# Block-sparse attention and a gated feed-forward layer on one core: weight rows in whole transfers, later loads in one piece, a new order

## The chip, the cores and the metric

The kernel runs on one core of one Trainium2 chip. A core has a tensor engine (PE, with its weight load shown apart as PEld), a vector engine (DVE), a scalar engine (ACT), GpSimd (POOL) and SyncE (SP), and sixteen DMA engines that serve all of them. The metric is the device time of one execution in microseconds (us). Three runs of the kernel before took 331.52, 333.68 and 333.03 us: the median is 333.03.

## The reference

```python
# q, k, v: (4, 8, 768, 64) f32: batch, heads, sequence, head size; blocks of 32
scores = scale * np.matmul(q, k.transpose(0, 1, 3, 2))
mask = np.abs(blk_i - blk_j) <= 1          # neighbours
mask = mask | (blk_i == 0) | (blk_j == 0) | (blk_i == n_blocks - 1) | (blk_j == n_blocks - 1)
for qb in range(n_blocks):                  # and three sampled blocks for each block of queries
    for kb in sampled_blocks[qb]:
        mask[qb*32:(qb+1)*32, kb*32:(kb+1)*32] = True
attn = softmax(np.where(mask, scores, -1e9))
x = np.matmul(attn, v)  # -> (3072 tokens, 512)
gate = 1.0 / (1.0 + np.exp(-(x @ w_gate)))  # w_gate, w_val: (512, 1536)
out = gate * (x @ w_val) @ w_out            # w_out: (1536, 512), out: (3072, 512) f32
```

## The kernel before

**Attention.** The four batches follow one another. For each, q, k and v are loaded with a cast from f32 to f16 into a ring of five staging buffers (`stg`). Such a cast is asked of POOL's DMA queue (q0 in the profile). Batch 0's are cut in few pieces; for batches 1 to 3 `load` (L551) cuts each of the three into `LPARTS = 4` transfers of two heads, 192 KB each as written. From batch 1 on k and q are put in row order by a copy on POOL or DVE (L726, L728); q's load is issued after k's copy, since the ring has no more room (L732). PE transposes k and q (L747, L750), and ACT and DVE evict them into `KT` and `QT` (L760, L765, L767). v is put in row order by DVE (L777) and stored to scratch in DRAM (`scr`, L786, on SP's queue from batch 1 on). From there windows of neighbouring blocks (L819) and the sampled blocks (L892, three gathers of 32 KB for each block of queries, on SP's queue, with registers for the block numbers) come back into `V1` and `V2`. The first and last block are held in `FL` and copied in (L831, L833).

A step handles two blocks of queries for all eight heads: POOL gathers their keys into `KG` (L868, L879), PE computes the scores (L912 for the mask, L919), DVE the maxima (L928), ACT the exponentials (L940), DVE the reciprocals (L947) and DVE or ACT the scaling (L960, L963); PE transposes the weights (L974), ACT or DVE evicts them (L980), PE multiplies by V (L993), and ACT or DVE evicts to `XA` (L1009, L1014). Eleven steps make a batch; the first and last block, which see all keys, are four dense units (L648, L1044 to L1098).

**Feed-forward.** The 24 tiles of 128 tokens are taken in seven groups: groups 0 and 1 have two tiles each, all of batch 0; group 2 has the last two tiles of batch 0 and the first two of batch 1; and so on. For each of twelve slices of 128 of the 1536 columns PE makes a gate matmul and a value matmul of four each (L1136, over the four parts of 128 of the 512 inputs), ACT takes tanh (L1144), and DVE combines (L1149). Then twelve matmuls with `wo` make a tile of the output (L1171), evicted at L1178 or L1180 and stored on SP's queue (L1185).

**Weights.** `weights` (L570) loads `wg` and `wv` in four column chunks of 384 columns, each in two transfers of 192 KB as written (L580), gate and value in turn; then `wo` in three parts of two transfers (L589). A gate matmul of a slice waits for the gate and the value chunk that hold that slice (L1139, L1141).

**The order.** All work is a list of operations with engines, costs, dependencies, buffers to take and to give back, and a priority. A planner (`Planner.run`, L196) sets them in order by list scheduling: for each engine the operation that can begin first, and among those about equal the one of lowest priority number. The kernel then issues the operations in that order, each engine in its own. `OFFSETS` shifts priorities by kind of operation, batch and quarter of the batch; `PREP` says when a batch's preparation comes; `DENSE` when the dense units. `GATES` names weight transfers that are issued only after the gathers of a block of batch 0 have been issued; `LGATE` does so for the loads of a batch, which wait for the gathers of that block of the batch before (L1107 to L1111). `FETCH` is what the planner reckons for one piece of PE's code while POOL's queue is loaded and while it isn't. Where PE has nothing to do before 60 us the planner puts in dummy matmuls (L1205).

Of the kernel before, what the change touches and what calls it, by code (L numbers as in the profile page):

```python
# [33 lines left out]
PREP = [-50.0, 0.26, 10.34, 20.82]  # L34


GATES = {0: 4, 4: 9, 6: 5, 8: 9}


LGATE = {1: 18, 2: 11, 3: 13}  # L40
# [27 lines left out]
}  # L68


def kind(o):

# [99 lines left out]
class Planner:  # L172
# [8 lines left out]
    LANES = 8  # L181


    PIECE, FIRST, FETCH = 256, 150, {True: 5.2, False: 3.5}

    def __init__(self):
        self.ops = []
# [167 lines left out]
def kernel(  # L355
# [15 lines left out]
    def pin(x):  # L371
        return tc.keep_in_program_order(x)
# [883 lines left out]
```

## Time and profile before

| | |
|---|---|
| median of three runs | 333.03 us |
| the profiled execution | 332.75 us |
| its span, first to last instruction | 331.0 us |
| PE busy | 311.0 us (94%) |
| DVE busy | 237.1 us (72%) |
| ACT busy | 219.0 us (66%) |
| POOL busy | 127.4 us (38%) |
| mean granted clock of PE | 0.983 |
| q0 (POOL's queue) | 17984 packets, 16.39 MB |
| q1 (SP's queue) | 24628 packets, 24.83 MB |
| q8 (PE's code) | 36 packets, 0.59 MB |

Busy tenths cut the span in 40 equal slices of 8.3 us; a digit is the busy share in tenths. "PEclk" is the granted clock of PE in tenths. In tables of stretches the share of DMA adds up the queues, so that it can pass 1. A row of the timeline or of waits names the engine and line that waited and, behind an arrow, what released it. The chain of waits is followed back from the last instruction; "issue" there is time in which nothing that the profile shows was waited for. Times to landing run from the issue of a transfer to its completion. The profile is of one execution, and the sums are made against its 332.75 us; 1.75 of them lie outside the span.

### The profile page before, as it was taken

The numbers are of one execution on the slowest core, as the hardware profiler recorded it, in microseconds if no ns is written. First come the engines' busy times: TensorE is split into PE (matmuls) and PEld (weight loads), VectorE is DVE, ScalarE is ACT, GpSimd is POOL, SyncE is SP. The second block draws the span as 40 slices with busy tenths as digits, with TensorE's granted clock in tenths as the row PEclk, the third lists the DMA queues.
The fourth block names the chain that finished last, engine by engine and source line by source line (L and its number), as shares of the span: only waits on it lengthen the run. The fifth ranks groups of instructions, "written<-read, shape, count | busy, mean of one in ns | idle before, by whom it ended". The sixth has DMA issues, their size and how long they took to land.

```text
span 331.0 us, 12430 instructions
## 1 busy us (share of the span) xinstructions
PE 311.0 (94%) x4574; PEld 188.7 (57%) x4574; DVE 237.1 (72%) x533; ACT 219.0 (66%) x656; POOL 127.4 (38%) x373
## 2 busy tenths in 40 slices
PE   6988898897997999999999999999999999999996
PEld 2545577766855746655556565655655665444443
DVE  3399987853697898998899976788987986304310
ACT  2156987854569999875895975759988765223322
POOL 6497786555445666443462433152221000000000
PEclk9999999999898799999999999999999999999999
DMA  7959999978523979524369742462223310020002
GB/s 112 216 174 220 224 225 234 214 195 186 155 73 90 188 175 213 133 65 143 113 136 220 172 107 97 126 171 63 69 64 105 108 35 0 2 95 32 0 34 95
DMA packets 42672, 42.00 MB, mean 127 GB/s; under 512 B 6931, under 2 KB 38804, under 8 KB 42612
## 3 DMA queue, kind: packets, MB, share of 16 engines
q0 software_dynamic: 17984, 16.39, 30.3%
q1 hardware_dynamic: 24628, 24.83, 25.8%
q8 instruction: 36, 0.59, 0.8%
q14 instruction: 24, 0.20, 0.2%
HBM read 45.97 MB, written 9.44 MB: 167 GB/s over the span
## 4 chain that ended last, share of the span: by engine, by line
PE 74%; DVE 13%; ACT 7%; issue 3%; DMA 2%; SPq 0%; DVEq 0%; ACTq 0%
PE bank L1136 32%; PE bank L1171 18%; ACT P L940 4%; PE bank L993 4%; PE bank L974 4%; PE twin L919 3%; PE twin L1205 3%; DVE NM L928 2%; DVE HT L1149 2%; DMA V<-scr 2%; DVE P L963 2%; PE twin L912 2%; DVE V L831 1%; PE bank L1081 1%; PE bank L750 1%
## 5 line engine op out<-in xcount | busy, mean ns | idle before, releaser
L940 ACT ACTIVATE P<-twin,NM 128x256 f16<-128x256 f32 x176 | 81.5, 489 | 15.1 <-DVE NM L928 14.9
L1149 DVE SCALAR_TENSOR_TENSOR HT<-TH,bank 128x512 f16<-128x512 f32 (+1 forms) x84 | 51.1, 609 | 41.7 <-PE bank L1136 37.7
L1136 PE MATMUL bank<-XA,wv 128*128 128x512 f16 (+1 forms) x336 | 77.1, 352 | 1.6 <-issue 1.1
L1136 PE MATMUL bank<-XA,wg 128*128 128x512 f16 (+1 forms) x336 | 77.0, 352 | 0.2 <-ACT XA L1009 0.2
L868 POOL COPY KG<-KT 128x64 f32 x264 | 51.4, 246 | 57.2 <-PE twin L919 50.6
L1144 ACT ACTIVATE TH<-bank 128x512 f32<-128x512 f32 (+1 forms) x84 | 45.8, 546 | 31.8 <-PE bank L1136 30.7
L1171 PE MATMUL bank<-wo,HT 128*128 128x512 f16 (+1 forms) x300 | 64.8, 370 | 0.3 <-DVE YS L1178 0.3
L928 DVE TENSOR_REDUCE NM<-twin 128x4 f32<-128x1024 f32 x44 | 52.5, 1218 | 3.2 <-PE twin L919 1.9
L1136 PEld LDWEIGHTS <-wv 128*128 128x128 f16 x336 | 31.7, 99 | 27.4 <-issue 2.5
L1171 PEld LDWEIGHTS <-HT 128*128 128x128 f16 x300 | 28.7, 98 | 30.5 <-issue 0.6
L1136 PEld LDWEIGHTS <-wg 128*128 128x128 f16 x336 | 30.5, 99 | 22.7 <-issue 1.2
L940 ACT ACTIVATION_READ_ACCUMULATOR P<-twin,NM 128x1 f32 x176 | 39.0, 221 | 0.0
L963 DVE TENSOR_SCALAR P<-P,ZZ 128x256 f16<-128x256 f16 x134 | 32.1, 301 | 1.5
L993 PEld LDWEIGHTS <-V 128*128 128x128 f16 x704 | 26.3, 100 | 11.4 <-issue 5.2
L974 PEld LDWEIGHTS <-P 128*128 128x128 f16 x352 | 22.8, 99 | 9.8 <-issue 3.5
L974 PE MATMUL bank<-ident,P 128*128 128x128 f16 x312 | 24.7, 222 | 2.1 <-ACT XA L1009 0.8
L833 POOL COPY V<-FL 32x768 f32<-32x768 f32 (+1 forms) x18 | 16.0, 922 | 26.6 <-PE bank L993 13.5
L993 PE MATMUL bank<-PTS,V 128*128 128x64 f16 x512 | 21.9, 197 | 4.5 <-DMA V<-scr 2.3
L1180 ACT ACTIVATE YS<-bank 128x512 f32<-128x512 f32 (+1 forms) x15 | 8.5, 569 | 21.9 <-PE bank L1171 21.9
L960 ACT ACTIVATE P<-P,ZZ 128x256 f16<-128x256 f16 x42 | 19.1, 520 | 4.3 <-DVE ZZ L947 4.1
L980 DVE COPY PTS<-bank 128x1024 f16<-128x1024 f16 x25 | 17.1, 685 | 5.3 <-PE bank L974 5.3
L919 PE MATMUL twin<-KG,QT 64*32 64x160 f16 x704 | 19.1, 238 | 0.0
(88 smaller groups left out, 394.1 us busy)
## 6 DMA issues: line engine op xcount, KB each, us to landing
V<-scr SPq DMA_DIRECT2D x264, 32.0 KB, 2.7
out_dram<-YS SPq DMA_DIRECT2D x23, 256.0 KB, 2.1
V<-scr SPq DMA_DIRECT2D x14, 288.0 KB, 4.3
stg<-in_v_dram POOLq DMA_DIRECT2D x12, 192.0 KB, 5.3
stg<-in_k_dram POOLq DMA_DIRECT2D x12, 192.0 KB, 7.5
scr<-stg SPq DMA_DIRECT2D x3, 768.0 KB, 3.4
stg<-in_q_dram POOLq DMA_DIRECT2D x12, 192.0 KB, 6.6
V<-scr SPq DMA_DIRECT2D x6, 384.0 KB, 4.2
```

Of the source, the lines that this page charges most:

```text
L868: pin(nc.gpsimd.tensor_copy(t[:, :, 1 + n], KW[r][:, :, bass.ds(vals[(i % 8) * 3 + n], BLK // 2)]))
L919: pin(nc.tensor.matmul(t[hh][cs, u, c0:c1], QT[r][rs, p, BLK * i : BLK * i + BLK], src, start=False, stop=True, skip_group_check=True))
L928: pin(nc.vector.tensor_reduce(NM[o.slots[hz][1]][:, 0:4], t, axis=AX.X, op=ALU.max, negate=True))
L940: pin(nc.scalar.activation(pb[:, u, :], t[:, u, :], AF.Exp, bias=NM[z][:, x : x + 1], scale=1.0, accum_out=ZZ[z][:, x : x + 1]))
L960: pin(nc.scalar.activation(pb[:, u, :], pb[:, u, :], AF.Copy, scale=ZZ[z][:, 2 * hh + u : 2 * hh + u + 1]))
L963: pin(nc.vector.tensor_scalar(pb[:, u, :], in0=pb[:, u, :], scalar1=ZZ[z][:, 2 * hh + u : 2 * hh + u + 1], scalar2=None, op0=ALU.mult))
L974: pin(nc.tensor.transpose(t[:, c * 128 : c * 128 + 128], pb[:, c * 128 : c * 128 + 128], ident))
L993: pin(nc.tensor.matmul(t[:, u, p, :], vt[:, ws, p * 128 : p * 128 + 128], pt[:, u, c, :, 32 * p : 32 * p + 32], start=(c == 0), stop=(c == ...
L1136: pin(nc.tensor.matmul(t, wt[:, c, f_ * 128 : f_ * 128 + 128], XT[g][:, c, :], start=(c == 0), stop=(c == 3)))
L1144: pin(nc.scalar.activation(TH[o.slots[ht][1]][:, 0:n], banks[o.slots[hg][1]][:, 0:n], AF.Tanh, bias=0.0, scale=0.5))
L1149: pin(nc.vector.scalar_tensor_tensor(HT[:, f_, hoff : hoff + n], in0=TH[o.slots[ht][1]][:, 0:n], scalar=1.0, in1=banks[o.slots[hv][1]][:, ...
L1171: pin(nc.tensor.matmul(t, HT[:, f_, hoff + tt * 128 : hoff + tt * 128 + 128], wo[:, f_, cols], start=(f_ == 0), stop=(f_ == NF - 1)))
```

## The change

Gate and value weights are loaded by whole rows: for each of the four parts of 128 inputs, one transfer of 128 rows of 1536 columns (384 KB as written), first the four of `wg` and then the four of `wv`. Every gate matmul then waits for all eight, and every value matmul for the four of `wv`, since each slice of columns needs all four parts. `wo` is loaded in three transfers of 512 KB. Each of q, k and v of batches 1 to 3 is loaded in one transfer of 768 KB. The planner's costs for these and for code pieces are set anew, and so are `GATES`, `LGATE`, one value of `PREP` and many of `OFFSETS`, so that the order of the work on each engine is another.

```diff
-PREP = [-50.0, 0.26, 10.34, 20.82]
-GATES = {0: 4, 4: 9, 6: 5, 8: 9}
-LGATE = {1: 18, 2: 11, 3: 13}
+PREP = [-50.0, 0.26, 10.34, 20.76]
+GATES = {1: 6, 2: 7, 4: 9, 5: 7, 6: 5}
+LGATE = {1: 14, 2: 11, 3: 14}
...
 OFFSETS = {
...
-    PIECE, FIRST, FETCH = 256, 150, {True: 5.2, False: 3.5}
+    PIECE, FIRST, FETCH = 256, 150, {True: 7.0, False: 3.6}
...
-    WCH, WOH = 4, 3
+    WOH = 3
...
-    LPARTS = 4
-
...
                 if name == "v":
-                    pin(nc.gpsimd.dma_start(v_head(t)[:, z], src[b].rearrange("h (p j) d -> p h j d", j=VJ)[:, z]))
+                    pin(nc.gpsimd.dma_start(v_head(t), src[b].rearrange("h (p j) d -> p h j d", j=VJ)))
...
-        n = NF // WCH
-        for ch in range(WCH):
-            c0, c1 = ch * n * 128, (ch + 1) * n * 128
-            for nm, t, src in (("wg", wg, moe_w_gate), ("wv", wv, moe_w_val)):
-                def f(o, t=t, src=src, c0=c0, c1=c1):
-                    for z in (slice(0, 2), slice(2, 4)):
-                        pin(nc.gpsimd.dma_start(t[:, z, c0:c1], src[:, c0:c1].rearrange("(c p) n -> p c n", p=128)[:, z]))
-                prev = P(f"{nm}{ch}", "POOL", 1.5, f, prio=-30, dma=8.8 / WCH, ndma=2, after=[prev])
+        for nm, t, src in (("wg", wg, moe_w_gate), ("wv", wv, moe_w_val)):
+            for ch in range(4):
+                def f(o, t=t, src=src, ch=ch):
+                    pin(nc.gpsimd.dma_start(t[:, ch, :], src[ch * 128 : ch * 128 + 128, :]))
+                prev = P(f"{nm}{ch}", "POOL", 0.75, f, prio=-30, dma=6.8 / 4, after=[prev])
                 FF["gate"].append(prev)
-                for ff in range(ch * n, ch * n + n):
-                    res[nm, ff] = prev
+            FF[nm] = FF["gate"][-4:]
         n = NF // WOH
         for ch in range(WOH):
             def f(o, r0=ch * n, r1=ch * n + n):
-                for z in range(r0, r1, 2):
-                    pin(nc.gpsimd.dma_start(wo[:, z : z + 2, :],
-                                            moe_w_out[z * 128 : z * 128 + 256, :].rearrange("(c p) n -> p c n", p=128)))
-            prev = P(f"wo{ch}", "POOL", 1.6, f, prio=-30, dma=9.4 / WOH, ndma=2, after=[prev])
+                pin(nc.gpsimd.dma_start(wo[:, r0:r1, :],
+                                        moe_w_out[r0 * 128 : r1 * 128, :].rearrange("(c p) n -> p c n", p=128)))
+            prev = P(f"wo{ch}", "POOL", 0.85, f, prio=-30, dma=9.4 / WOH, after=[prev])
...
-            ldv, hv = load("v", v, b, pp - 0.050, ldeps, LPARTS)
-            ldk, hk = load("k", k, b, pp - 0.049, ldv[-1:], LPARTS)
-            ldq, hq = load("q", q, b, pp - 0.048, ldk[-1:], LPARTS)
+            ldv, hv = load("v", v, b, pp - 0.050, ldeps)
+            ldk, hk = load("k", k, b, pp - 0.049, ldv)
+            ldq, hq = load("q", q, b, pp - 0.048, ldk)
...
-                  deps=xdeps + [w["wg", f_], w["wv", f_]], prio=pr, count=4, ...
+                  deps=xdeps + FF["wg"] + FF["wv"], prio=pr, count=4, ...
-                   deps=xdeps + [w["wv", f_], a], prio=pr, count=4, ...
+                   deps=xdeps + FF["wv"] + [a], prio=pr, count=4, ...
```

More of the change, by code (lines that the diff above doesn't have):

```diff
@@ L558, in f @@
                 t = stg[pl.handles[h][1]]
-                z = QPARTS[x] if tokens else slice(x * n, x * n + n)
                 if name == "v":
-                    pin(nc.gpsimd.dma_start(v_head(t)[:, z], src[b].rearrange("h (p j) d -> p h j d", j=VJ)[:, z]))
+                    pin(nc.gpsimd.dma_start(v_head(t), src[b].rearrange("h (p j) d -> p h j d", j=VJ)))
                     return
                 t, y = by_head(t), src[b].rearrange("h (p j) d -> p h j d", j=TJ)
+                z = QPARTS[x] if tokens else slice(x * n, x * n + n)
                 pin(nc.gpsimd.dma_start(t[z], y[z]) if tokens else nc.gpsimd.dma_start(t[:, z], y[:, z]))
             res.append(P(f"ld{name}{b}{x}", "POOL", 0.8, f, after=list(after) + res[-1:], prio=prio,
-                         acq=[(h, stages)] if x == 0 else [], lat=LATE[0] if b else None, dma=4.4 * (QPARTS[x].stop - QPARTS[x].start) / TP if tokens else 4.4 / parts))
+                         acq=[(h, stages)] if x == 0 else [], lat=LATE[0] if b else None, dma=3.4 * (QPARTS[x].stop - QPARTS[x].start) / TP if tokens else 4.4 / parts))
         return res, h
@@ L1138 @@
             a = P(hg, "PE", n * 0.00168, lambda o, f_=f_, h=hg, fn=f_mm: fn(o, f_, h, wg),
-                  deps=xdeps + [w["wg", f_], w["wv", f_]], prio=pr, count=4, acq=[(hg, pg_of(g)), (ht + "t", [("ff", x) for x in range(len(pg_of(g)) // 3)])])
+                  deps=xdeps + FF["wg"] + FF["wv"], prio=pr, count=4, acq=[(hg, pg_of(g)), (ht + "t", [("ff", x) for x in range(len(pg_of(g)) // 3)])])
             b_ = P(hv, "PE", n * 0.00168, lambda o, f_=f_, h=hv, fn=f_mm: fn(o, f_, h, wv),
-                   deps=xdeps + [w["wv", f_], a], prio=pr, count=4, acq=[(hv, pg_of(g))], rel=[ht + "t"])
+                   deps=xdeps + FF["wv"] + [a], prio=pr, count=4, acq=[(hv, pg_of(g))], rel=[ht + "t"])
             def f_th(o, hg=hg, ht=ht, n=n):
```

47 rows, old and new, of the table OFFSETS are left out of this document.

## The prediction

> **What bounds the kernel now.** I read the busy tenths of the page first, then busy time by stage, then the chain of waits, the DMA queues by stage, and the timelines of POOL and SyncE.
>
> ```profile
> PE   6988898897997999999999999999999999999996
> PEclk9999999999898799999999999999999999999999
> DMA  7959999978523979524369742462223310020002
> ```
>
> PE is busy nearly throughout; its gaps, and both dips of the granted clock, lie in the first 15 slices of 8.3 us. DMA is full from slice 4 to slice 8 (25 to 66 us). By stage:
>
> ```profile
> 46.00:64.00 18.00, 15.82 (x354) 13.10 (x354) 14.18 (x36) 14.27 (x56) 12.73 (x41) 1.00 1.24 227
> ...
> 78.00:86.00 8.00, 5.75 (x51) 4.48 (x50) 1.88 (x6) 2.07 (x8) 5.19 (x17) 0.79 0.69 209
> ...
> 101.00:114.00 13.00, 9.88 (x294) 8.27 (x268) 11.03 (x27) 11.85 (x42) 9.88 (x32) 0.74 0.78 151
> ...
> 130.00:278.00 148.00, 147.64 (x2306) 88.17 (x2305) 126.53 (x277) 115.48 (x357) 46.71 (x159) 1.00 0.44 111
> ```
>
> The columns are the stretch, its length, busy time of PE, PEld, DVE, ACT and POOL, granted clock, DMA share (queues added) and GB/s. From 130 us on PE has nothing to give back: what is lost or won there must come from more or less work, and the change has none. The recoverable time lies ahead of it: 2.2 us idle in 46 to 64; 2.25 idle and 21% of the clock over 8 us (1.7) in 78 to 86; 3.1 idle and 26% over 13 us (3.4) in 101 to 114. That is some 12.7 us. Before 46 us PE waits for the first attention steps and is kept warm by 82 dummy matmuls (L1205); DVE is busy 24.4 of the 26 us from 20 to 46 and sets that pace.
>
> Why PE stands at 78 and 101:
>
> ```profile
> 59.09 1.05 issue
> ...
> 74.77 5.70 DMA V<-scr
> ```
> ```profile
> SPq L786 <- DVE P L963: 8.0, 1, 8.0
> ```
> ```profile
> 59.65 2.53 POOL L564 DMA_DIRECT2D stg<-in_k_dram  x4
> 69.52 1.90 POOL L726 COPY stg<-stg 96x2048 f32<-96x2048 f32 x1 [7.34 <-DVE P L963]
> 71.36 2.50 POOL L564 DMA_DIRECT2D stg<-in_q_dram  x4
> ```
>
> Batch 1 comes late. Its v is issued from 54.4 to 59.7 and lands about 65.3; SyncE holds the store of the shuffled v (L786) for 8.0 us, and behind it, in order, stand the last gathers of batch 0: a gather issued at 74.8 lands 5.7 us later and PE stands 2.25 us for it (the 78 to 86 hole). Batch 1's k lands about 69.4 (last quarter issued by 62.2, median 7.2 to landing), is shuffled at 69.52, q is issued behind that and shuffled at 81.21, and batch 1's first scores run at 91.1. By 101 the gate and value matmuls of groups 0 and 1 are used up, and those of group 2, which needs batch 1's tiles, begin at 113.6: the second hole.
>
> **The change, part by part.**
>
> *Weight rows.* The price of a packet, from the queue views of three stretches:
>
> ```profile
> q0 software_dynamic: 283, 0.90, 91.8%
> ...
> q0 software_dynamic: 1353, 0.98, 106.1%
> ...
> q0 software_dynamic: 1026, 0.88, 111.1%
> ```
>
> These are 23 to 27, 36 to 42 and 62 to 67 us. Share x length x 16 engines / packets gives 208 ns at 3.2 KB (V windows, no cast), 75 ns at 0.72 KB (weights, with some 4-byte completions) and 87 ns at 0.86 KB. In the packet records a 768 B weight piece takes 79 ns at the median and a 1 KB piece of k 97, so 18 ns for each further 256 B. A whole row is 3072 B written, so 97 + 8 x 18 = 241 ns is my estimate; ends 208 (the uncast row) and 316 (four times 79: no gain). Gate and value weights are 4096 pieces now, 4096 x 79 / 16 = 20.2 us of all engines; 1024 rows at 241 are 15.4. Saved: 4.8 us of a stage where DMA is full (0 to 6.9).
>
> *The new gate.* Every gate or value matmul now waits for all eight row transfers, where now the first needs two column chunks. The weights flow from about 28.3 us (mean packet size falls from 3.2 to 0.7 KB there) at q0 shares of about 1.05: 28.3 + 20.2/1.05 = 47.5 now, 28.3 + 15.4/1.05 = 43 after, and 1.5 us to the landing: 44.5. The first of these matmuls runs at 46.33 now, set by attention, so I cost the gate at nothing; its cover is 1.8 us. Without it (rows at 316 ns) they land at 49, a loss of up to 2.7. Queued behind a waiting matmul on PE would be batch 0's attention, hence the bound counts in full.
>
> *POOL's issues.* 16 weight issues at 0.71, 6 of wo at 0.70 and 36 quarter loads at 0.67 become 8, 3 and 9; the rows of larger transfers are 0.73 (384 KB, batch 0's k) and 0.92 (768 KB, its v), so 39.7 us become about 16. POOL is not the bound (50.6 us of its idle is waiting for score matmuls), and I count nothing for this by itself, but q of batch 1 is issued in one go of about 0.7 to 0.9 us and not in 2.5.
>
> *Batch 1 earlier.* Behind the weights in the same queue stand wo (1536 x 97/16 = 9.3 us), v (1024 x 79/16 = 5.1) and k (768 x 97/16 = 4.7), 19.1 in all. At 0.95 of the engines: 47.5 + 20.1 + 1.7 = 69.3, which is where k lands now, and 64.8 after. The gate on the loads moves from the gathers of block 18 to those of block 14, the eleventh block, gathered by about 41 us, so the loads can stand in the queue before wo is done. k, its shuffle, q and its shuffle come 4.5 us earlier, q 1 to 2 more for its single issue: 4.5 to 6. The SyncE store of v comes about 5 earlier, and with it the gathers behind it. The start of group 2 moves from 113.6 by about 5, since PE had slack there and DVE (11.0 of 13) and ACT (11.9 of 13) are what the first steps of batch 1 go by. Gain 5 us (0 to 12.7, the whole recoverable time). What is late next is those steps themselves on ACT and DVE.
>
> *Batches 2 and 3.* Same single transfers; PE is full there, so nothing (worth 0 either way while PE has work from earlier groups).
>
> *Longer packets beside others.* Small gathers landed in 6.4 us (median of 6) beside the 3.2 KB packets of 23 to 27 and in 4.5 (of 10) beside the 0.72 KB ones of 36 to 42. PE's code comes through the same engines: 36 pieces of 16 KB (q8), one per 254 PE instructions (9148/36). From 45.6 to 63.8 they came every 6.1 us, and PE stood for them in the middle of a run, 1.1 us at 52.9 and 1.05 at 59.1 ("issue"). Under weight rows, from 28 to 43, gathers and code may come 1.9 us later. The dummy matmuls and the DVE pace cover it in part: the third step's PV ran at 41.7, while its gathers were issued by 30. I take 0.5 us (0 to 3 there).
>
> The Trainium skill, DMA: Bandwidth & Descriptors, "Queues, rings and completion order", says that each engine takes turns between queues only at packet boundaries. It speaks against this change, and the 6.4 against 4.5 us agrees with it. By that rule alone the 1.9 us would stand once in full on the way to the first gate matmul, and the sum would be 330 where mine is 328.
>
> *The order.* Engine orders are replanned as a whole and can't be seen here; ±4 us, the size of one hole of the two.
>
> **Sum.** 332.75 (the profiled execution; span 331.0) - 5 + 0.5 = 328.25, say 328. The runs' median of 333.03 is 0.3 above the profiled one, which alters nothing. 1% is 3.3 us, about what can be told from no change.
>
> **Rivals.**
>
> *Code late (slower).* Place: 46 to 68, where PE already goes by its code pieces. If larger transfers hold each back by a further 1.9 us (the gathers' difference), four pieces cost 7 us, part regained from batch 1: 332.75 + 7 - 3 = 336 to 337. It decides once the spacing of pieces there exceeds 6.1 us. For: PE's two stalls lie exactly there. Against: by then the rows have landed, and wo and the loads keep their 1 KB and 768 B packets.
>
> *All weights too late.* Rows no faster than pieces: 2.7 lost at 46 and nothing gained for batch 1: 335. For: a cast row of 3 KB stands nowhere in the trace. Against: 208 ns for 3.2 KB uncast.
>
> *Hidden anyway.* Batch 1 is earlier, but ACT (11.9 of 13) holds its first steps, or the order gives the gain back: 330 to 335.
>
> *A new hole.* The new order lets PE run dry once more as from 101 to 114 (6.5 us), after 114, where nothing of batch 0 is left to fill it, and keeps 2 of the gain: 332.75 + 6.5 - 2 = 337. For: the planner counts costs, not this chip's waits. Against: PE idles 0.4 us in 148 from 130 on, with the gate work of a whole group in hand.
>
> *All of it.* Both holes close, the clock stays up, and the order uses it: 320 to 323.
>
> **Chances.** Forecast (325 to 331) 0.42; all of it 0.10; hidden 0.09; weights too late 0.05; code late 0.19; a new hole 0.15. Faster by over 1% (below 329.7) is all of "all of it" and 0.36 of the forecast: 0.46. Within 1%: the rest of the forecast, hidden, and a little of the weights and of code late: 0.18. Slower (above 336.3): 0.36. For 8 in 10 I leave out the near end of "all of it" beyond 321 and what lies above 339; that takes in the lost cover of the gate, code late, a new hole and most of the recoverable 12.7. Both signs hold much of the chance; the likeliest case's own range is 325 to 331.
>
> **What would show it.** Right: the weight packets at 3 KB and near 241 ns; the last weight landed by 45 and the first gate matmul by 47; batch 1's k shuffle near 65 and its first scores near 86; no clock dip near 82; group 2's first gate matmul near 108. Wrong: rows near 316 ns, code pieces over 6.1 us apart between 46 and 68 with "issue" on PE, or PE below full after 130.

## The result and the profile after

The changed kernel takes 334.04 us (median of 20 runs), the kernel before 331.81 in the runs beside it: a ratio of 1.0052, 95% interval 1.0027 to 1.0078. The ratio leaves out executions more than 1.5% above their kernel's fastest, so by it the change is slower by about 1.7 us and not by the 2.2 of the medians. 328 had been forecast; the measured change is inside the 1% that was named as about what can be told from no change. The profiled execution of the changed kernel took 336.02 us (span 334.1), 2 us above the median of its runs, which lie between 331.4 and 336.6, so single gaps below are read for what they are and not added up to the microsecond.

The page after, busy tenths in 40 slices of 8.35 us:

```profile
PE   5997697899899898999999979999999999999996
PEclk9999999999999999999999999999999999999999
DMA  7959999979329991434397934533223020020002
```

Both dips of the granted clock are gone (slices 11, 13 and 14 before), as forecast. That holds for this execution, whose mean granted clock was 0.998; over the twenty the mean lies between 0.990 and 1.000, mostly at 0.995, and over 25 of the kernel before, the base of e13 to e16, between 0.978 and 0.995. One stretch of 3.41 us at half clock, as the kernel before has one from 81.1 us on, takes 0.005 off the mean. But PE's row has new weak slices: the first, the fourth and the fifth, and slice 24, around 195 us, where the kernel before had nothing but nines. By stage, with the columns as before (stretch, length, busy time of PE, PEld, DVE, ACT and POOL, granted clock, DMA share, GB/s):

```profile
46.00:64.00 18.00, 15.52 (x344) 11.57 (x344) 15.42 (x41) 16.73 (x58) 3.89 (x14) 1.00 1.23 227
78.00:86.00 8.00, 6.92 (x83) 4.83 (x84) 4.93 (x8) 4.66 (x11) 3.49 (x3) 1.00 0.64 172
101.00:114.00 13.00, 12.96 (x178) 7.92 (x174) 10.70 (x27) 12.00 (x37) 2.83 (x13) 1.00 1.15 213
114.00:130.00 16.00, 14.09 (x262) 9.25 (x259) 12.62 (x26) 12.70 (x37) 9.18 (x31) 1.00 0.71 170
130.00:278.00 148.00, 144.13 (x2148) 83.78 (x2146) 121.40 (x273) 108.10 (x310) 41.12 (x142) 1.00 0.43 108
```

The two holes of before have closed: 78 to 86 went from 5.75 busy at a clock of 0.79 to 6.92 at 1.00, and 101 to 114 from 9.88 at 0.74 to 12.96 at 1.00. From 130 us on, where PE had been busy 147.64 of 148 us, it now stands for 3.9. What PE waits for from 110 to 200 us (engine, line and what released it: us in total, times, longest):

```profile
PE twin L1062 <- DVE DP L1053: 1.7, 1, 1.7
PE bank L741 <- POOL stg L720: 1.0, 1, 1.0
PE bank L1130 <- DVE HT L1143: 0.9, 1, 0.9
PE bank L741 <- DVE stg L722: 0.6, 1, 0.6
```

Lines of the changed kernel are six below those of the kernel before, up to the end of the file: L1130 is the gate and value matmul (L1136 before), L987 the product with V (L993), L913 the scores (L919), L720 GpSimd's copy of k or q into row order (L726), L862 the copy of keys (L868), L1053 the scaling of a dense unit (L1059). The four waits come, in this order, at 194, 115, 133 and 129 us.

The early part lost too. In the chain that leads to 54 us, pieces in order of time (start, us, what):

```profile
25.36 8.30 DMA V<-scr
...
38.31 0.10 PE twin L913 x11
38.40 1.56 issue
39.96 0.36 PE twin L913 x14
```

PE waits 1.33 us for the gather that takes 8.30 us to land, and stands 1.56 us in the middle of a run of scores: a piece of its code had come at 37.45 to 38.39. The stand ends 1.6 us after that piece's packet; others like it end 1.2 to 1.5 us after theirs, at 54.0 and 60.1 us in the kernel before, at 52.6 in the changed one and at 49.9 in e9. From 24 to 50 us the kernel before has neither wait. Milestones of five kernels, read from the first gate matmul of a group of tiles (the columns on the right are experiments, below):

| us | before | after | a third of the weights (e9) | short copies (e11) | both (e13) |
|---|---|---|---|---|---|
| first gate matmul | 46.3 | 49.0 | 46.3 | 48.5 | 46.5 |
| first scores of batch 1 | 91.2 | 86.9 | | | |
| group 2 begins | 113.6 | 110.4 | 108.2 | 108.9 | 107.6 |
| group 3 | 164.5 | 163.9 | 159.3 | 161.2 | 158.1 |
| group 4 | 210.8 | 213.0 | 208.4 | 209.7 | 205.6 |
| span | 331.0 | 334.1 | 329.4 | 330.2 | 326.1 |

So the changed kernel starts 2.7 us late, is 3.2 ahead at group 2, 0.6 ahead at group 3 and 2.2 behind at group 4. A milestone of one order doesn't stand for the same work done as in the other; PE's idle time, which "The sum, mended" adds up below, doesn't have this fault. The same early part also differs from execution to execution: in the changed kernel, e11, e14, e15 and e16, which are alike up to 68 us, the first gate matmul comes at 48.1 to 49.5. The question for the experiments is what makes the start late, and what takes the lead of group 2 away.

### The profile page after: what moved, and what is told of

The parts are those of the page before. It is cut to its first block, busy times and chain, and to the rows that moved or that the text cites. A ratio compares the mean times of both kernels' runs of the same rounds, so it can differ in the third digit from the quotient of the medians.

```text
span 334.1 us, 12372 instructions
## 1 busy us (share of the span) xinstructions
PE 310.6 (93%) x4577; PEld 186.9 (56%) x4577; DVE 236.1 (71%) x539; ACT 221.0 (66%) x647; POOL 103.0 (31%) x338
## 4 chain that ended last, share of the span: by engine, by line
PE 65%; DMA 12%; DVE 7%; ACT 7%; issue 4%; SPq 3%; POOL 1%; POOLq 0%; DVEq 0%; ACTq 0%
PE bank L1130 30%; PE bank L1165 14%; PE bank L987 4%; PE bank L968 4%; DMA V<-scr 4%; DMA stg<-in_q_dram 3%; ACT P L934 3%; SPq L886 3%; PE twin L913 3%; PE twin L1199 2%; PE twin L906 2%; DVE V L825 1%; DMA scr<-stg 1%; DMA out_dram<-YS 1%; DMA FL<-scr 1%
## 5 line engine op out<-in xcount | busy, mean ns | idle before, releaser
L1130 PE MATMUL bank<-XA,wv 128*128 128x512 f16 (+1 forms) x336 | 76.0, 348 | 2.3 <-DVE HT L1143 2.1
L862 POOL COPY KG<-KT 128x64 f32 x264 | 50.0, 243 | 90.7 <-PE twin L913 84.4
L1130 PE MATMUL bank<-XA,wg 128*128 128x512 f16 (+1 forms) x336 | 76.1, 349 | 1.0 <-ACT TH L1138 0.4
L1130 PEld LDWEIGHTS <-wv 128*128 128x128 f16 x336 | 31.4, 98 | 27.7 <-issue 3.2
L1130 PEld LDWEIGHTS <-wg 128*128 128x128 f16 x336 | 29.6, 98 | 23.1 <-issue 2.7
L957 DVE TENSOR_SCALAR P<-P,ZZ 128x256 f16<-128x256 f16 x146 | 36.8, 313 | 1.5
L987 PEld LDWEIGHTS <-V 128*128 128x128 f16 x704 | 26.1, 98 | 12.2 <-issue 5.9
L1174 ACT ACTIVATE YS<-bank 128x512 f32<-128x512 f32 (+1 forms) x19 | 10.9, 572 | 30.0 <-PE bank L1165 28.0
L987 PE MATMUL bank<-PTS,V 128*128 128x64 f16 x624 | 26.1, 193 | 3.1 <-DMA V<-scr 2.2
L968 PEld LDWEIGHTS <-P 128*128 128x128 f16 x352 | 22.2, 98 | 10.1 <-issue 2.9
L827 POOL COPY V<-FL 32x768 f32<-32x768 f32 (+1 forms) x20 | 18.5, 953 | 21.4 <-PE bank L987 13.2
L974 ACT COPY PTS<-bank 128x1024 f16<-128x1024 f16 x18 | 18.2, 1013 | 7.8 <-PE bank L968 7.7
L913 PE MATMUL twin<-KG,QT 64*32 64x160 f16 x704 | 19.2, 234 | 2.7 <-issue 2.7
L720 POOL COPY stg<-stg 96x2048 f32<-96x2048 f32 x5 | 9.4, 1890 | 38.6 <-PE bank L1075 16.8
```

The lines of the kernel that those rows point to most:

```text
L827: pin(nc.gpsimd.tensor_copy(dst.bitcast(f32), src.bitcast(f32).broadcast_to([BLK, n, DM // 2])))
L862: pin(nc.gpsimd.tensor_copy(t[:, :, 1 + n], KW[r][:, :, bass.ds(vals[(i % 8) * 3 + n], BLK // 2)]))
L913: pin(nc.tensor.matmul(t[hh][cs, u, c0:c1], QT[r][rs, p, BLK * i : BLK * i + BLK], src, start=False, stop=True, skip_group_check=True))
L957: pin(nc.vector.tensor_scalar(pb[:, u, :], in0=pb[:, u, :], scalar1=ZZ[z][:, 2 * hh + u : 2 * hh + u + 1], scalar2=None, op0=ALU.mult))
L968: pin(nc.tensor.transpose(t[:, c * 128 : c * 128 + 128], pb[:, c * 128 : c * 128 + 128], ident))
L987: pin(nc.tensor.matmul(t[:, u, p, :], vt[:, ws, p * 128 : p * 128 + 128], pt[:, u, c, :, 32 * p : 32 * p + 32], start=(c == 0), stop=(c == ...
```

## The experiments

Each run stands against runs of the kernel before on the same chip; ratios are to those, with 95% intervals. Where a run is set against the changed kernel, its ratio is divided by 1.0052; the intervals of both then count. The theories at the start were: the longer packets or transfers cost time by themselves (A, C); the order is what costs or gains (B); or both only in one another's company.

### Parts of the change, one at a time

**e1: the new order, weights in short packets.** The same eight transfers, cut by columns, so that packets are 768 B. Cut so, the first gate matmul and the first value matmul each wait for one transfer (landed at 33.7 and 43.2 us), so the new gate is out of this run as well.

```diff
-pin(nc.gpsimd.dma_start(t[:, ch, :], src[ch * 128 : ch * 128 + 128, :]))
+pin(nc.gpsimd.dma_start(t[:, :, ch * 384 : ch * 384 + 384],
+                        src[:, ch * 384 : ch * 384 + 384].rearrange("(c p) n -> p c n", p=128)))
```

> The changed kernel in its own order, its eight weight transfers of 384 KB kept in number and size, but each a chunk of 384 columns of all four parts, so that its packets are 768 B and not 3072 B as written. Theory A (long weight packets hold back the gathers and PE's code of batch 0, and move no more bytes per us): gathers issued from 28 to 36 us land in about 5.0 us and not 6.5, PE's 1.3 us wait for a gather at 33.8 goes, the first gate matmul comes 1 to 2 us before 49.0, and the time falls by 1 to 2.5 us, to about 332. Theory B (the new order is the cost, not the packets): the time stays at 334 within 0.7. The step of the prediction that rows are faster: the weights would take 4 to 5 us longer, the first gate matmul would come at 53 or so and the time would rise by 2 to 4.

1.0108 (1.0073 to 1.0142): 0.5% slower than the changed kernel, not faster. Its gathers of 28 to 36 us land in 5.1 us at the median, against 6.5 in the changed kernel, and the 1.33 us wait is gone, but the stand for code is still there (1.56 us at 37.2) and the first gate matmul comes at 49.5. In between lies a dip of the clock. The same six dummy matmuls, in the changed kernel and in e1:

```profile
40.71 1.46 PE L1199 MATMUL bank<-ident 128*128 128x512 f16 x6
```
```profile
39.65 2.77 PE L1199 MATMUL bank<-ident 128*128 128x512 f16 x6
```

Up to there e1 is 1.1 us ahead; from 39.4 to 42.8 us the granted clock stands at half, and the lead is gone. So long packets are what makes the gathers slow and not what makes the code late; whether the start would come earlier without them, this execution doesn't show. The run's time doesn't hang on such a dip alone: an execution at a mean clock of 0.999 took 336.25.

**e2: the new order, later loads in four transfers each.**

```diff
-pin(nc.gpsimd.dma_start(v_head(t), src[b].rearrange(...)))
+for y in range(4 if b else 1):     # two heads each; k and q likewise
+    pin(nc.gpsimd.dma_start(v_head(t)[:, s], src[b].rearrange(...)[:, s]))
```

> The changed kernel in its own order, but q, k and v of batches 1 to 3 each loaded in four transfers of 192 KB as before, issued one after the other at the same place. Theory C (single transfers of 768 KB are what delays batches 2 and 3): batch 2's q, issued at 116.3, lands in about 9 us and not 11.6, PE's idle time from 114 to 136 shrinks by 1 us or more, and the time falls by 1 to 2 us. Theory A and theory B: nothing but POOL's extra issue time of about 1.7 us for a load, so the time stays at 334 within 0.7, or rises by up to 1.

1.0071 (1.0045 to 1.0098), the same as the changed kernel within the intervals. Whole loads neither gain nor cost there.

**e3: the old order, later loads whole**, each issued in the place of its first quarter.

```diff
+if b:
+    if x:
+        return
+    z = slice(0, H)
```

> The kernel before in its own order, but q, k and v of batches 1 to 3 each loaded in one transfer of 768 KB, issued where the first quarter stood. Theory C: 1 to 2 us slower than before, ratio 1.003 to 1.006. Theories A and B: the same within 0.7 us, or a little faster, since POOL has 1.7 us less to issue for each load: ratio 0.997 to 1.001.

1.0022 (0.9982 to 1.0062): no difference that this can tell.

**e4: the old order, weights by rows.** Each of its eight weight operations issues one whole row transfer.

```diff
-for z in (slice(0, 2), slice(2, 4)):
-    pin(nc.gpsimd.dma_start(t[:, z, c0:c1], src[:, c0:c1].rearrange("(c p) n -> p c n", p=128)[:, z]))
+c = c0 // 384
+pin(nc.gpsimd.dma_start(t[:, c, :], src[c * 128 : c * 128 + 128, :]))
```

> The kernel before in its own order, but its eight weight operations each load one whole row of 1536 columns (one transfer of 384 KB with 3072 B packets, not two of 192 KB with 768 B), gate and value in turn; every gate matmul then needs all eight. Theory A: the gathers slow as in the changed kernel (6.5 us), the last weights land at 48 to 50, the first gate matmul, set at 46.3, waits until then and holds batch 0's attention behind it on PE: 2 to 4 us slower, ratio 1.006 to 1.012. Theory B: the gate falls in PE's slack, ratio within 1.002. The step of the prediction that rows are faster: the last weights land by 45, nothing waits, and the time falls by up to 2 us.

1.003 (1.0004 to 1.0057). Gathers of 28 to 36 us land in 8.0 us at the median where they took 5.0, those of 36 to 43 in 7.5 where they took 4.5. That agrees with the rule on turns at packet boundaries that the prediction cites from the Trainium skill (DMA: Bandwidth & Descriptors, "Queues, rings and completion order"). What PE waited for from 24 to 50 us:

```profile
PE twin L993 <- DMA V<-scr: 2.2, 2, 1.3
PE twin L648 <- ACT P L940: 0.8, 1, 0.8
```

The kernel before has no such DMA wait. The first gate matmul comes at 49.6, 3.3 us later (49.1 in e5, which has the same rows), but group 2 at 114.8, only 1.2 later, and some 1 us reaches the end. The old order has slack between these two points.

**e5: the old order with all the new transfers** (rows, `wo` in three, whole loads: the edits of e3 and e4, and one transfer for each part of `wo`).

> The kernel before in its own order with all of the changed transfers: rows, wo in three of 512 KB, and whole loads of batches 1 to 3. Theory F (the transfers cost all of the 0.5% and the new order nothing): the two single costs found add up, 1.002 and 1.003, so ratio 1.004 to 1.008, the same as the changed kernel. Theory G (the new order costs): ratio 1.000 to 1.003. If the new order is what the new transfers need and regains something: above 1.008.

1.0045 (1.0013 to 1.0078): as much above the kernel before as the changed kernel is. In the old order the transfers alone cost as much as the whole change; that is the same size, and not yet the same cause.

**e6: the new order with all the old transfers** (the weights in sixteen, `wo` in six, the loads in quarters).

> The changed kernel in its own order with all of the old transfers: weights in sixteen of 192 KB with 768 B packets, wo in six, loads of batches 1 to 3 in quarters. It differs from the kernel before by the order alone. Theory F: ratio 0.998 to 1.002. Theory G: ratio 1.005 or more; the two single results in this order, 1.011 and 1.007 against 1.005 for the changed kernel, add up to 1.013.

1.0215 (1.0158 to 1.0271). In this order the old transfers are worse by 1.6%, and POOL's timeline shows why. The changed kernel:

```profile
35.74 2.13 POOL L576 DMA_DIRECT2D wv<-in_moe_w_val_dram  x4
37.82 2.28 POOL L583 DMA_DIRECT2D wo<-in_moe_w_out_dram  x3
40.03 2.18 POOL L862 COPY KG<-KT 128x64 f32 x12
```

And e6, rows of the same stretch:

```profile
35.77 4.93 POOL L580 DMA_DIRECT2D wv<-in_moe_w_val_dram  x7
40.93 0.70 POOL L580 DMA_DIRECT2D wv<-in_moe_w_val_dram  x1 [0.23 <-issue]
42.15 0.71 POOL L588 DMA_DIRECT2D wo<-in_moe_w_out_dram  x1 [0.52 <-DMA wv<-in_moe_w_val_dram]
...
47.90 0.70 POOL L588 DMA_DIRECT2D wo<-in_moe_w_out_dram  x1 [0.39 <-DMA wv<-in_moe_w_val_dram]
48.59 1.10 POOL L867 COPY KG<-KT 128x64 f32 x6
```

With the old transfers POOL issues weights until 48.6 us, twice as many and those of `wo` each behind an earlier one's landing, and the copies of keys that stand behind them in its order come 8.6 us later. PE stands 4.38 us for them, until 49.2, the granted clock is at half from 49.5 to 56.3, and the first gate matmul comes at 55.3 instead of 49.0.

**e7 and e8: other orders from the same transfers.** The kernel before with only the planner's costs of a code piece of the changed one, and the reverse.

```diff
-PIECE, FIRST, FETCH = 256, 150, {True: 5.2, False: 3.5}
+PIECE, FIRST, FETCH = 256, 150, {True: 7.0, False: 3.6}      # e7; e8 the other way round
```

> The kernel before with one constant of the planner altered: a piece of PE's code is reckoned at 7.0 and 3.6 us, as in the change, not 5.2 and 3.5. The transfers are the old ones; from the early part on the order is another. It measures what a new order by itself moves. If orders that the planner makes are all about as good: ratio 0.997 to 1.003. If an order is fitted to the chip by its priorities, and any other is worse: 1.005 to 1.02.

> The changed kernel with that constant put back to 5.2 and 3.5 us: new transfers, another order. If orders are about as good: ratio to the kernel before 1.002 to 1.008, as the changed kernel's 1.005. If each order is fitted: 1.01 to 1.025.

1.0179 (1.0123 to 1.0235) and 1.0319 (1.0255 to 1.0384); e8 is 2.7% above the changed kernel. But for a few dummy matmuls no instruction's work differs; the planner sets another order with priorities that were set for the first. This is the size of the order as a term by itself: 2 to 3%, more than the whole change.

### What the new order runs into

**e9 and e10: a third of the weights' bytes**, in the new and in the old order. Every engine does the same work; the matmuls use the columns that are there three times over.

```diff
-pin(nc.gpsimd.dma_start(t[:, ch, :], src[ch * 128 : ch * 128 + 128, :]))
+pin(nc.gpsimd.dma_start(t[:, ch, 0:512], src[ch * 128 : ch * 128 + 128, 0:512]))
...
-wt[:, c, f_ * 128 : f_ * 128 + 128]
+wt[:, c, f_ % 4 * 128 : f_ % 4 * 128 + 128]
```

> The changed kernel, each gate and value transfer cut to its first 512 of 1536 columns (a third of the bytes, packets of 1 KB written), and the gate and value matmuls use these 512 columns three times over: two thirds of both weight matrices do not enter the result, the work of every engine is the same. Theory A, the weights' transfers delay what comes before the first gate matmul: the gathers issued from 28 to 43 us land in about 5 us, the DMA waits in the chain at 25 to 40 us go, the first gate matmul comes at 46 to 47 where the changed kernel has 49.0, and the time falls by 2 to 4 us, to about 330. Theory B, the new order with its 85 dummy matmuls and the pace of the vector engine set that start: first gate matmul at 48.5 or later, time within 1 us of the changed kernel's 334. Under both the holes after 114 us stay (they have another cause).

> The kernel before, each gate and value transfer cut to the first 128 columns of its 384 (a third of the bytes, packets of 256 B written), and the gate and value matmuls use those columns three times over: two thirds of both weight matrices do not enter the result, the work of every engine is the same. It is the counterpart of the run beside it. Theory A, only the 3 KB rows cost something: the kernel before gains less than 1 us. Theory A2, any weight traffic costs it: the kernel before gains as much as the changed kernel does, 2 to 4 us, and the rows themselves are not the difference. Theory B: both stay within 1 us.

The new order: 0.9968 (0.9935 to 1.0000), 0.84% below the changed kernel. The old: 0.998 (0.995 to 1.001). The first gate matmul of the new order moves from 49.0 to 46.3, the 1.33 us for a gather shrinks to 0.34, and the stand for code at 38.4 is gone (the code piece of that place is there at 35.1 us where it was at 38.4). So the delay ahead of the first gate matmul comes with the weights' traffic. Packets are shorter here too, 1 KB and not 3, so this run by itself doesn't part bytes from length; by e1 short packets rid PE of the wait for the gather and not of the stand for code. The old order carries nearly the same traffic (219 against 225 GB/s from 28 to 48 us, below) and is touched by it little; its group 2 begins between 112.0 and 114.8 us in the kernel before, e3, e4, e5, e10 and e12 alike. The expectation was wrong in one point: the holes after 114 did not stay. At 194 us there is none, because the copy and the operation beside it no longer fall together (the copy ends at 190.7, as the scaling begins). So the 0.84% isn't the price of the late start alone.

**e11 and e12: GpSimd's copies of k and q cut to a quarter**, in the new and in the old order.

```diff
-pin(nc.gpsimd.tensor_copy(d.bitcast(f32), t.bitcast(f32).rearrange("p h j d -> p j h d")))
+pin(nc.gpsimd.tensor_copy(d.bitcast(f32)[:, 0:2], t.bitcast(f32).rearrange("p h j d -> p j h d")[:, 0:2]))
```

> The changed kernel, the copies on GpSimd that put k and q of batches 1 to 3 in row order cut to two of eight rows per partition, so that each takes about 0.5 us in place of 1.9; the other rows of k and q keep what stood in the buffer, so the scores of batches 1 to 3 are not the reference's. Theory H, these copies hold vector operations that run beside them (1.98 us for an operation that takes 0.42 elsewhere, and the idle stretches at 115, 128 and 194 us): those stretches shrink to below 0.5 us each, and the time falls by 2 to 3.5 us. Theory E, the idle stretches come from elsewhere and the copy's length is covered: time within 1 us of the changed kernel's 334. In either case q comes 1.4 us earlier, since its load waits for the copy of k.

> The kernel before with the same edit, the counterpart of the run beside it: the copies on GpSimd of k and q of batches 1 to 3 cut to two of eight rows per partition, the scores of batches 1 to 3 so not the reference's. Theory H, only the new order lets these copies meet vector operations at a bad place: the kernel before gains less than 1 us, and what it gains is at 78 to 114 us, where batch 1's k and q come late. Theory E: both kernels gain about the same.

The new order: 0.9986 (0.9949 to 1.0024), 0.66% below the changed kernel. The old: 1.0049 (1.0015 to 1.0082), no gain at all, but 0.5% slower with less work to do. So shifts of half a per cent can come from timing alone, and the 0.66% is to be read beside that; the timelines say more. At 194 us in the changed kernel, two timelines, DVE's and POOL's:

```profile
193.54 0.15 DVE L1052 RECIPROCAL ZZ<-ZZ 128x1 f32<-128x1 f32 x1
193.73 1.98 DVE L1053 TENSOR_SCALAR DP<-DP,ZZ 128x768 f16<-128x768 f16 x1
195.64 0.85 DVE L1003 CAST XA<-bank 64x256 f16<-64x256 f32 x2
```
```profile
193.61 1.89 POOL L720 COPY stg<-stg 96x2048 f32<-96x2048 f32 x1 [2.89 <-DMA stg<-in_q_dram]
```

The copy ends at 195.5, and the scaling 0.2 us later. At 115 us it is the same with k's copy, in part (DVE, then POOL):

```profile
115.29 1.27 DVE L1053 TENSOR_SCALAR DP<-DP,ZZ 128x768 f16<-128x768 f16 x1
```
```profile
114.46 1.89 POOL L720 COPY stg<-stg 96x2048 f32<-96x2048 f32 x1 [9.88 <-DMA stg<-in_k_dram]
```

All sixteen of these scalings, the changed kernel first, then e11 (duration in ns, least, median and greatest, and where):

```profile
L1053 DVE TENSOR_SCALAR DP<-DP,ZZ x16: 419/421/1983, 28.6 to 249.0; 128x768 f16<-128x768 f16 x16
```
```profile
L1053 DVE TENSOR_SCALAR DP<-DP,ZZ x16: 419/420/602, 28.3 to 245.7; 128x768 f16<-128x768 f16 x16
```

In the kernel before the greatest is 621 ns: there no such scaling fell beside a long copy. PE's stretches in e11:

```profile
114.00:130.00 16.00, 15.52 (x210) 10.02 (x208) 12.97 (x29) 13.84 (x40) 7.51 (x31) 1.00 0.75 166
130.00:278.00 148.00, 145.62 (x2189) 84.35 (x2188) 119.70 (x277) 109.49 (x316) 37.69 (x141) 1.00 0.43 108
```

PE wins 1.4 and 1.5 us in them.

**e13: both edits, of e9 and of e11, together.**

> The changed kernel with a third of the gate and value weights (two thirds of both matrices do not enter the result) and the copies of k and q on GpSimd cut to two of eight rows, both edits as in the runs before. If the two are separate costs of the new order, they add: 2.8 + 2.2 = 5 us below the changed kernel's 334, about 329, ratio to before about 0.990; the first gate matmul at 46.3, group 2 at about 107. If they are one cost seen twice (a later start that the later holes then inherit), the time is that of the weights alone, about 331.3.

329.22 us, 0.9908 (0.9868 to 0.9948), as expected of two separate costs: they add up to 1.43% where 0.84 and 0.66 were measured alone. Its busy row and the stretch from 130 us:

```profile
PE   6998997899899999999999999999999999999995
```
```profile
130.00:278.00 148.00, 147.09 (x2183) 85.31 (x2176) 121.65 (x283) 111.56 (x323) 37.05 (x140) 1.00 0.40 106
```

Slice 24 is a nine again and PE stands 0.9 us in 148. The time is 1.2 us above the 328 of the forecast, but with two thirds of the weights' bytes gone, which the forecast had not taken away.

**e14 and e15: the copies of q alone, those of k alone**, in the new order. No load waits for q's copy; q's load waits for k's.

```diff
+c = 2 if nm in "q" else TJ          # e15: "k"
-pin(nc.gpsimd.tensor_copy(d.bitcast(f32), ...))
+pin(nc.gpsimd.tensor_copy(d.bitcast(f32)[:, 0:c], ...[:, 0:c]))
```

> The changed kernel with only q's copies on GpSimd cut to two of eight rows (q of batches 1 and 3; q of batch 2 is copied by the vector engine); the scores of these batches are not the reference's. No load waits for these copies. Theory H, the copy holds vector operations: the 1.7 us at 194 us goes, since the scaling beside it takes 0.42 us in place of 1.98, and the holes at 115 and 129 stay; time 1 to 1.7 us below 334. Theory L, the copies cost by making q's load late: nothing changes, 334.

> The changed kernel with only k's copies on GpSimd cut to two of eight rows (all of batches 1 to 3; their scores are not the reference's). q's load comes 1.3 us earlier. Theory H: the hole at 115 shrinks (scaling 0.6 us in place of 1.27) and the one at 194 stays; time 0.5 to 1.2 us below 334. Theory L: q lands 1.3 us or more earlier, the holes at 115, 129 and 194 go, and time falls by the whole 2.2 us, to about 332.

q alone: 1.0013 (0.9972 to 1.0054), 0.4% below the changed kernel, which the intervals don't tell from nothing. k alone: 0.997 (0.9916 to 1.0024), 0.8% below. In e14 the wait at 194 us is gone, as the holding of vector operations has it, and the one for k's copy at 115 stays at half its length; what is left of PE's waits from 110 to 200 us, but for two of 0.2 us (lines are one further down):

```profile
PE bank L742 <- POOL stg L721: 0.5, 1, 0.5
PE bank L1131 <- DVE HT L1144: 0.3, 1, 0.3
```

The wait at 129 is gone as well, which that theory did not expect: q of batch 2 landed at 123.4 and not at 127.9, more than the 1.3 us of the shorter copy can move, so executions differ here by as much as the effect. In e15 those at 115, 129 and 194 are all gone, as expected of copies that cost by making q late; its q of batch 2 landed at 125.7, and no scaling took more than 0.42 us. Both mechanisms are seen at work, and the intervals are too wide to share out the 2.2 us between them. The changed kernel's trace shows k's copy doing both: it holds the scaling beside it at 115 us, and q's load is issued at 116.3, as it ends.

**e16: the dense scaling in another form**, with all of the computation.

```diff
-pin(nc.vector.tensor_scalar(d, in0=d, scalar1=z[:, 1:2], scalar2=None, op0=ALU.mult))
+y = d.rearrange("p (n j) -> p j n", j=VJ) if b else d
+pin(nc.vector.tensor_scalar(y, in0=y, scalar1=z[:, 1:2], scalar2=None, op0=ALU.mult))
```

> The changed kernel with the whole computation; only the scaling of the dense rows by the vector engine (128x768, f16) goes through its elements with a stride of six from batch 1 on. The Trainium skill, SBUF — State Buffer, says that only a vector operation in a two-port mode, or with two inputs from SBUF, is locked out by GpSimd. In 0.42 us it takes 768 elements a partition, faster than one a cycle, so it may be such a mode. Theory H with that rule: the scaling takes 0.8 to 1.0 us everywhere, no longer 1.98 beside the copy at 194 us or 1.27 at 115; the holes there shrink by about 1 and 0.3 us, and the time falls by 0.5 to 1 us. Without that rule it is still held beside the copy and elsewhere twice as long: time 0 to 1 us above 334.

343.37 us, 1.0302 (1.0195 to 1.0409). The expectation fell twice.

```profile
L1054 DVE TENSOR_SCALAR DP<-DP,ZZ x16: 420/1519/2652, 28.3 to 259.9; 128x768 f16<-128x768 f16 x16
```

The strided form takes 1.52 us, not 0.8 to 1.0, and is held all the same: the 2.65 us stand at 117.0, beside a copy that ends at 118.3. The Trainium skill, VectorE: DVE Perf Modes, "What auto-detection actually checks", asks no unit step of the two-port mode. That fits the holding; which mode the strided form ran in no run shows, and its 2 ns for an element are far from the 0.55 of the plain form. But the run is worth having for its price: twelve operations that take 1.1 us longer on DVE, 13 us of an engine that is busy 71% of the time, cost some 8 us at the end (2.5%, from four executions between 341.6 and 346.4). That suggests that DVE has little slack in the new order.

## Why the prediction was wrong

Two steps failed above all: the weight rows were to save 4.8 us, and batches 2 and 3 were to cost nothing. One sum of the chances doesn't come out: slower than 336.3 has 0.36, while the two rivals that end above it, code late and a new hole, have 0.34 together; nothing here hangs on that.

**Weight rows: the price of a packet was right, the saving was not.** A row of 3072 B took 247 ns at the median, for which 241 had been estimated. But 4.8 us were to be saved by dividing packet times by sixteen engines, and the packets of one engine overlap: the shares of the queues add up to 1.28 of what sixteen engines have. DMA queues of the stretch 28 to 48 us (packets, MB, share of 16 engines), before and after:

```profile
DMA packets 5879, 4.38 MB, mean 219 GB/s; under 512 B 712, under 2 KB 5854, under 8 KB 5873
...
q0 software_dynamic: 4328, 3.20, 103.0%
```
```profile
DMA packets 2725, 4.51 MB, mean 225 GB/s; under 512 B 537, under 2 KB 1653, under 8 KB 2719
...
q0 software_dynamic: 1371, 3.45, 88.5%
```

A third as many packets fill 88.5% where 103% stood, and yet the bytes of all queues flow 3% faster only. The weights' first packet to their last took 21.9 us before and 19.9 after, a gain of 2.0. SP's queue moved 0.40 MB less in that time (0.99 MB against 1.39), which is 1.8 us at 222 GB/s, so next to nothing is left for the rows. The last weight landed at 48.8 us and not at 44.5. A rate of some 220 GB/s fits as the limit of this stage, in both kernels and in e1 (220, with 768 B packets); what sets it no run shows. The share of busy time, which the prediction took for the limit, is not a limit when it can fall at the same rate. The trace of the kernel before had it already: by the prediction's working its weights end at 47.5 us, and their last packet ends at 50.2.

**The new gate** cost nothing, as forecast, but by luck: the weights landed at 48.8, the first gate matmul ran at 49.0 and the value matmul that needs the last row at 49.8, with no wait of PE ahead of them. (In the instructions a gate matmul waits for the four rows of `wg`, and the value matmul right behind it for the four of `wv`.) Had attention come as early as in the kernel before, 46.3, PE would have stood some 1.7 us for the last row. The forecast cover of 1.8 was gone; the late start hid it.

**POOL's issues** were counted at nothing, because POOL has 50 us of idle time. That step failed: idle time elsewhere doesn't help the copies of keys that stand right behind the issues. e6 is 1.62% above the changed kernel, some 5.4 us. Short packets alone (e1) cost 0.56% of it and quarter loads alone (e2) 0.19%, so about half, 2.9 us, is left for the doubled issues of weights and for what the three do together; no run has the issues alone. The term was in neither the sum nor the rivals.

**Batch 1: the effect as forecast, by another way.** Its first scores were to come near 86 us and came at 86.9; group 2 was to begin near 108 and began at 110.4; both clock dips went. But k's copy was to run near 65 us, and k landed only at 68.6 (69.3 before), though it had been issued by 52.1 and not by 62.2. The rows brought batch 1 almost nothing. q, in one transfer, was copied 2.0 us earlier (79.2 against 81.2), and the first scores came 4.3 earlier; the rest is the new order. That they came when forecast is luck. The gain by group 2 is 3.2 of the 5 us.

**Batches 2 and 3: nothing, was the step that failed most.** "PE is full there" was read from the kernel before, as a property of the stage. It was a property of that order. In the new one GpSimd's copies of k and q, whose place in time goes by when a load lands, fell beside vector operations, and PE stood for the copy at 115 us and for the held scaling at 194. PE's idle time from 114 us on went from 3.9 to 9.0 us; e11 prices the copies at 2.2 us (0.66%). This is the rival of a new hole after 114, which had a chance of 0.15 and was priced at 6.5 us; what speaks for it was named as the planner's blindness, and the place, as it turned out, was the planner's rule that keeps some vector operations off these copies by planned times, not real ones. The Trainium skill, SBUF — State Buffer, "Who interferes with whom", says that GpSimd and a vector operation in a two-port mode lock each other out for a whole instruction; the 1.98 us against 0.42 agrees.

**Longer packets beside others: 0.5 us taken, 2.7 measured at the first gate matmul** (2.4 of PE's idle time up to 78 us), within the bound of 3. The mechanism was half right: a gather of 8.30 us and a late code piece, for which PE stands at 32 to 40 us. "Code late" had been looked for at 46 to 68, where the spacing did grow to 6.3 to 7.5 us, with one stand of 1.13 us where the kernel before has two. The gather's part goes with the packets' length (e1, e4); the stand for code stays with short packets (e1) and goes with a third of the bytes (e9). How much of the late start is length and how much is bytes stays open. By the rule on turns at packet boundaries that the prediction cites from the Trainium skill (DMA: Bandwidth & Descriptors, "Queues, rings and completion order"), 1.9 us were to be lost here and 330 was the sum. The 2.4 us and the gathers of e4 (5.0 to 8.0 us) are nearer to that than to the 0.5 taken; the rest of the way to 334 is not of this stage.

**The order: ±4 us** was too narrow. e6 differs from the kernel before by the order alone and is 7 us slower (2.15%); e7 and e8 give 6 and 9 us for a slight change in the planner's costs. The changed kernel is 1.6% faster than its order with the old transfers and the same as the old order with the new ones (e5, 0.1% apart): a new order set for new transfers that came out even.

**The sum, mended.** PE is busy for nearly the same time in both kernels (311.0 and 310.6 us), so its idle time adds up to the difference, whatever the order. From the profiled executions, in us:

| PE idle | before | after | a third of the weights (e9) | short copies (e11) | both (e13) |
|---|---|---|---|---|---|
| up to 78 us | 10.1 | 12.5 | 11.2 | 12.0 | 10.1 |
| 78 to 114 us | 6.0 | 1.9 | 2.1 | 1.5 | 1.4 |
| from 114 us on | 3.9 | 9.0 | 5.8 | 6.1 | 4.2 |

The forecast had 0.5 us lost in the first row, 5 gained in the second and nothing in the third. Measured are 2.4 lost, 4.1 gained and 5.1 lost, 3.4 in all, where the spans differ by 3.1. The two edits of e13 together take both losses back, to 10.1 and 4.2, and keep the gain. Alone neither does: e9 takes only 1.3 of its gain in the first row and 3.2 in the third, since an earlier start also moves the copies against the vector operations, as at 194 us. What stays open is how the late start divides between the bytes of the weights and the length of their packets, and how the 2.2 us of the copies divide between holding and late loads. A buffer of its own for q, which would free its load from k's copy, was not tried. No experiment with the whole computation beat the kernel before.

## What to carry to other kernels

Read a DMA stage by the rate it reaches, not by its busy share: here packets on one engine overlapped, and fewer, longer ones lowered the share and left the rate where it was. Try the working first on the kernel that has already run. An engine's idle total says little about an instruction that stands right behind a row of DMA issues in that engine's order. And "PE is full there" is a property of one order: when the order changes, look again at every stage, and above all at what an engine does whose work begins when a transfer lands.

## What the hardware showed that had not been expected

- A GpSimd copy (96x2048 f32, 1.89 us) holds a 128x768 f16 scaling on the vector engine for as long as it runs: 1.98 us against 0.42, and likewise 2.07 and 2.06 in e1 and 1.93 in e2, each ending 0.2 us after its copy.
- The same scaling with a stride of six elements takes 1.52 us, 2 ns for an element, and is held beside the copy as well.
- From 28 to 48 us, 4328 packets of POOL's queue before and 1371 after, both with all else beside them, make 219 and 225 GB/s, while the summed share of the DMA engines goes from 1.28 to 1.10.
- Where the granted clock falls in these traces, it stands at half for 3.41 us or for 6.83 us (3.41 at 81.1 and 6.83 at 105.0 us in the kernel before, 3.41 at 39.4 in e1, 6.83 at 49.5 in e6).
